# Moving the kernel-tap products of a chunk behind the next chunk's Z groups, in pieces

## The chip, the cores and the metric

The kernel runs on one core of a Trainium2 chip. The time is device time of one execution in microseconds, as a median over runs; the profile is one execution, and its times are counted from the start of its span. Engines are named as in the profile: PE is TensorE (with PEld, its weight loads), DVE VectorE, ACT ScalarE, POOL GpSimd, SP the sync engine, which only issues DMAs.

## The reference

The forward and all gradients of a gated mix of two layers are computed for a sequence of L = 2048 positions, D = 448 channels, with x taken as a constant in the second layer:

```python
g = sigmoid((x * gate_w).sum(-1, keepdims=True))
# a: state space layer, N = 256 states per channel
P = exp(logdA[:, :, None] * l[None, None, :])        # D x N x L
K = einsum("dn,dnl,dn->dl", Cc, P, dB).real          # the taps of a long convolution
y = irfft(rfft(pad(u)) * rfft(pad(K)))[:L] + u * Dskip
# b: squared-ReLU MLP, F = 1792
h = relu(x @ w1 + b1); b = (h * h) @ w2 + b2
out = g * a + (1 - g) * b
```

The outputs are out and the gradients by u, the A, B, C, log_dt and Dskip parameters, w1, b1, w2, b2 and gate_w. What matters here is K: per channel a sum over 256 states of complex powers of one number per state, at 2048 positions; and the way back from dK, the gradient by the taps, to the states.

## The kernel before

**Stages.** Up to about 199 us the kernel loads, does the backward transforms of the convolution and computes dK. From 199 to 628 us a loop goes over the channels in chunks of 32 (`NCH` = 14, with one round more to finish); the MLP's matmuls run beside it. From 628 us the taps K, which the loop has stored to DRAM, are loaded again (L1172), the forward convolution follows (`fwd1`, matmuls at L231), then what is left of the MLP's backward and the weight gradients.

**One chunk.** The position index is split in a product of two tables of powers, X and Y. `x_pair` with `build_x` (VectorE, L762 to L767) makes the X tables of two chunks at once, in rounds with even c. `build_y(c, half)` (VectorE, L774, L775 and L777) makes the Y table in `Ys[c % 2]` by doubling; its operands are broadcast by ScalarE in `expand_y` (L809, L811), those of X in `expand_x` (L804, L805). The K products, `kgen` at L841, are 128 small matmuls per chunk: weights from Y, 128x64, moving data from X, 16 columns, four summed into each place of one PSUM tile `X` (psX). `k_out` (L849, ScalarE) copies the tile into the SBUF buffer KS; at chunks 9 and 13 GpSimd or ScalarE stores KS to DRAM (L855).

For the way back the tables are transposed: X by PE through psX with a ScalarE copy (`tables_t`, L867 and L868), Y by a transposing DMA on SP for three of four groups (`load_yt`, L887), by PE and ScalarE for the fourth (`turn_yt`, L879 and L880) and for the last chunk. `back_z` multiplies the dK block of a chunk (`dk_chunk`, L892) with a transposed Y group: 32 matmuls per group g at L910 into psF, a single buffer, and ScalarE converts the group to bf16 (L914). There are four groups, called Z0 to Z3 here. `back_p` multiplies Z by the transposed X on VectorE, two products of 128x2048 per half (L930), and PE sums them over channels into psS and psN3 (L939). A round c of the loop does Z and P of chunk c−1 and the tables and K of chunk c: K of chunk c is issued in the second half, behind `build_y(c, 1)` and ahead of the transposes of Y and of the second P.

**Beside it.** The MLP's forward hidden layer (`hidden`, L608 and L611, with ScalarE at L613 to L618), its projection (`project`, L1078 and L1080, ScalarE L1081, store L1082), transposes of the weights (L1104, L1115) and the backward through the MLP (`row_block`: L1143 and L1146 on PE, L1148 on ScalarE, product L1155 on VectorE, store L1156 by GpSimd) are issued after the loop in the program, and three of the four row blocks are there to fill the loop's holes.

**What sets the order.** The program is written in the order in which the tensors are produced; a scheduler orders each engine's instructions when the kernel is built, by dependences, priorities and a model of durations, and this order is then fixed. At run time each engine works through its own queue in that order, and waits at an instruction whose input or buffer is not ready. `tc.issue_after(ins)` adds an edge: what is issued in its scope comes behind `ins`. A PSUM tile of one tag (`X`, `S`, `N0` to `N3`, `F`) has one buffer, so that a tile's next use waits for the last reader of the one before. Also Y's two buffers and X's pair of tables may be written again only when K and the transposes of the chunk that they held have been read.

Of the kernel before, what the change touches and what calls it, by code (L numbers as in the profile page):

```python
# [19 lines left out]
P = 128  # L20
# [6 lines left out]
CW = 8  # L27
NG = 4
CC = NG * CW
NCH = D // CC  # L30
# [4 lines left out]
NA = 16  # L35
# [303 lines left out]
def kernel(ctx, tc, A_u, A_A_re, A_A_im, A_B_re, A_B_im, A_C_re, A_C_im, A_log_dt, A_Dskip,  # L339
# [4 lines left out]
    V, S, G_, T_ = nc.vector, nc.scalar, nc.gpsimd, nc.tensor  # L344
# [26 lines left out]
    K = Ker(tc, pool, psum)  # L371
# [140 lines left out]
    ps = K.ps("X", [P, FT + 4], bf16)  # L512
# [43 lines left out]
    th, s, q_ = Lr_, dsa[:, 0:2 * D], dsa[:, 2 * D:4 * D]  # L556
# [26 lines left out]
    ps = K.ps("S", [P, 512])  # L583
# [147 lines left out]
    Ys = [YA[:], KB[:, 6144:14336].rearrange("p (w t b) -> p w t b", t=2, b=64)]  # L731
    XB = K.t("X16", [P, 8192])
    XT5 = XB.rearrange("p (t k w a r) -> p t k w a r", t=2, k=2, w=W2, a=NA)
    XWs = [XT5[:, :, k] for k in range(2)]
# [92 lines left out]
                              PIY[:, k, ws].rearrange("p w t d -> p (w t) d"), rows=rows)  # L827
        return last

    def kgen(c):  # L830
        ps = K.ps("X", [P, 16 * NA])
        for i in range(CW):
            for gg in range(2):
                for jt in range(2):
                    g = 2 * jt + gg
                    ch = 8 * gg + i
                    k = 0
                    for h in range(2):
                        w = g * 16 + h * 8 + i
                        for t in range(2):  # L840
                            T_.matmul(ps[64 * jt:64 * jt + 64, ch * NA:ch * NA + NA], lhsT=Ys[c % 2][:, w, t, :], rhs=XWs[c % 2][:, 1 - t, w, :, 1],  # L841
                                      start=(k == 0), stop=(k == 3), tile_position=(0, 64 * jt))
                            k += 1
        return ps

    def k_out(c, ps):
        cp, cc = c // GC, c % GC
        kv = KS[:, :, cp].rearrange("p a (g q i) -> p q a g i", g=2, q=GC)[:, cc]
        S.copy(kv, ps[:].rearrange("p (g i a) -> p a g i", g=2, a=NA)[:, 0:VA])  # L849
        if c in (9, NCH - 1):  # L850
            c0, c1 = (0, 5) if c == 9 else (5, 7)
            for jt in range(2):
                for (a0, na, st_) in ((0, 2, 1), (2, 2, 2), (4, 2, 1), (6, 6, 256), (12, 1, 1)):
                    nb_ = 1 if a0 == 12 else 64
                    (nc.scalar if jt and c > 9 else G_).dma_start(bass.AP(tensor=k_d, offset=AOFF[a0] * D + 224 * jt + 32 * c0, ap=[[4 * D, nb_], [st_ * D, na], [1, 32 * (c1 - c0)]]),  # L855
                                 KS[64 * jt:64 * jt + nb_, a0:a0 + na, c0:c1].rearrange("p a c e -> p a (c e)"))

    def tables_t(c, gp):
        nonlocal xi
        XT = XTr[xi % 4].rearrange("p (t g n) -> p t g n", g=2, t=2)  # L860
        xi += 1
        pt = K.ps("X", [P, 4, 256], bf16)
        for t in range(2):
            for gg in range(2):
                for h in range(2):
                    w = (2 * gp + gg) * 16 + h * 8
                    T_.transpose(pt[:, 2 * t + gg, h * P:(h + 1) * P], XWs[c % 2][:, t, w:w + 8, :, 0].rearrange("p w a -> p (w a)"), ident[:])  # L867
        S.copy(XT.rearrange("p t g n -> p (t g n)"), pt[:].rearrange("p a n -> p (a n)"))  # L868
        return XT
# [22 lines left out]
        S.copy(DKs[:, c % 2, 0, :, :, 0:VA], src)  # L892
        S.activation(DKs[:, c % 2, 1, :, :, 0:VA], src, ACT.Copy, scale=brow[:, 0:1])

    def back_z(c, YTs, gs):

        nonlocal zi
        cc = c % GC
        DKc = DKs[:, c % 2]
        zb = Zr[zi % 2].rearrange("p (s t g n) -> p s t g n", t=2, s=2, g=2)  # L900
        zi += 1
        for gg, g in enumerate(gs):
            psz = K.psF()
            for s in range(2):
                for par in (1, 0):
                    for ii in range(4):
                        i = 2 * ii + par
                        m = (1 + par) * NA
                        for t in range(2):
                            T_.matmul(psz[32 * ii:32 * ii + m, t, 256 * s:256 * s + 256],  # L910
                                      lhsT=DKc[64 * t:64 * t + 64, s, g, 2 * ii:2 * ii + 1 + par].rearrange("p i a -> p (i a)"),
                                      rhs=YTs[g][64 * t:64 * t + 64, :, i, :], start=True, stop=True, tile_position=(64 * t, 32 * ii),
                                      skip_group_check=True)
            S.copy(zb[:, :, :, gg].rearrange("p s t n -> p t s n"), psz[:].rearrange("p t (s n) -> p t s n", s=2))  # L914
        return zb

    def back_p(c, XT, zb, gs, after):
# [38 lines left out]
    XTs, YTs = {}, {}  # L956
# [63 lines left out]
    for c in range(NCH + 1):  # L1020
        z01 = z23 = None
        if c == 0:
            x_next(0)
        elif c % 2 == 1 and c < NCH:
            XTs[c] = [tables_t(c, 0)]
        if 0 < c < NCH:
            YTs[c] = []
        if c > 0:
            z01 = back_z(c - 1, YTs[c - 1], (0, 1))
        if c % 2 == 1 and c < NCH:  # L1030
            XTs[c].append(tables_t(c, 1))
        if c > 0:
            z23 = back_z(c - 1, YTs[c - 1], (2, 3))
        ap = None
        for half in range(2):
            if c < NCH:
                if c > 0:
                    ay = build_y(c, half, ap or ay)
                if half == 1:
                    k_out(c, kgen(c))  # L1040
                for g in (2 * half, 2 * half + 1) if c > 0 else ():
                    YTs[c].append(turn_yt(c, g) if g == 3 or c == NCH - 1 else load_yt(c, g))
                if c + 1 < NCH:
                    if half == 0:
                        lry = load_ry(c + 1)
                        lry1 = lry if c == 0 else lry1
                        if c % 2 == 1:
                            expand_x(c + 1)
                            expand_x(c + 2)
                        if c == 0:  # L1050
                            expand_y(1, 0, 4)
                    elif c == 0:
                        expand_y(1, 4, 5)
                    else:
                        expand_y(c + 1)
# [42 lines left out]
    for jp in range(FT // 2):  # L1098
        ps = K.ps(NT[ni % 3], [P, 2, D], bf16)
# [8 lines left out]
    for jp in range(FT // 2):  # L1108
        ps = K.ps(NT[ni % 3], [P, DT, 2, P], bf16)
# [292 lines left out]
    gp = const.tile([P, LT], bf16, name="gp")  # L1402
# [121 lines left out]
```

## Time and profile before

| | |
|---|---|
| median of 5 runs | 926.98 us |
| runs | 929.69, 921.80, 932.99, 926.98, 924.27 us |
| the profiled execution | 929.69 us, of which its span is 927.2 us |
| 0 to 199 us (before the loop): PE, DVE, ACT busy | 115.22, 131.99, 131.70 us |
| 199 to 628 us (the loop): PE, DVE, ACT busy | 357.55, 355.59, 316.04 us |
| 628 to 927 us (behind it): PE, DVE, ACT busy | 246.42, 151.68, 144.73 us |
| K products, L841: one; a chunk's 128 | 0.176 us (they overlap); 2.2 to 3.6 us |
| copy of K, L849 | 0.332 us, 14 of them |
| conversion of a Z group, L914 | 1.025 us, 56 of them |
| product for P, L930 | 1.218 us |

How it is read: the page gives busy time over the whole span, and per slice; views of the trace give it for any stretch. A row of the timeline has the start, the duration, engine, line, operation, the tiles written and read, how many instructions were merged, and in brackets how long the engine had been idle before and what ended that. "L930 <- ACT R L914" in the waits reads: VectorE stood at L930 until ScalarE's L914 had written R. Granted clock (PEclk) is the share of TensorE's full clock. Only waits of the engine that is late in a stage cost time.

### The profile page before, as it was taken

Reading aid. Unit: us, or ns where it says so; the run is one execution under the profiler, and the core shown is the slowest. Engines: PE = TensorE matmul, PEld = TensorE weight load, DVE = VectorE, ACT = ScalarE, POOL = GpSimd, SP = SyncE. Lnnn points to the kernel's source line nnn. Section 1 sums busy time; section 2 is a strip of 40 time slices with the busy share of each in tenths; the row PEclk is TensorE's granted clock in tenths of the full one; section 3 lists DMA queues with packets and bytes.
Section 4 is the critical chain, followed back from the end, with each engine's and each line's share of the span. In section 5 each row is a group of like instructions: output and inputs, shape, how many; then the busy total and the mean of one; then the engine's idle time right before and its main releaser. Section 6 shows DMA issues by size and latency. Waiting matters only on the chain.

```text
span 927.2 us, 18872 instructions
## 1 busy us (share of the span) xinstructions
PE 719.2 (78%) x7600; PEld 345.5 (37%) x7633; DVE 639.3 (69%) x1034; ACT 592.5 (64%) x939; POOL 203.4 (22%) x352
## 2 busy tenths in 40 slices
PE   1876744657877877887989779789859869988795
PEld 0332222234334343343553443444323225443353
DVE  4675857696399999989795997933418949759200
ACT  2887768637968968798777836564516645554443
POOL 2341010103112112121221302224213013354120
PEclk8777566577888998897956779999979779989998
DMA  9797675896542656448455576549999988789772
GB/s 238 190 326 266 245 276 220 309 313 168 153 113 72 143 138 156 103 116 148 144 118 111 133 165 157 138 111 301 308 421 275 285 245 254 215 235 273 178 159 62
DMA packets 168238, 184.96 MB, mean 199 GB/s; under 512 B 95347, under 2 KB 145944, under 8 KB 167352
## 3 DMA queue, kind: packets, MB, share of 16 engines
q1 hardware_dynamic: 119062, 83.32, 36.4%
q0 software_dynamic: 21568, 67.46, 22.3%
q10 hardware_dynamic: 27522, 33.00, 11.0%
q8 instruction: 59, 0.97, 0.4%
q14 instruction: 27, 0.22, 0.1%
HBM read 89.60 MB, written 73.13 MB: 175 GB/s over the span
## 4 chain that ended last, share of the span: by engine, by line
PE 34%; ACT 20%; DMA 17%; issue 15%; DVE 9%; POOL 3%; ACTq 1%; POOLq 0%; DVEq 0%; SPq 0%
PE psN L1080 4%; PE psF L1229 3%; DMA R<-Y 3%; DMA S<-rT_d 2%; PE psX L841 2%; PE psF L910 2%; DMA P<-hd 2%; PE psX L879 2%; PE psN L608 2%; PE psN L1229 2%; ACT R L868 2%; DMA rec_d<-F 1%; PE psN L296 1%; ACT R L914 1%; PE psS L939 1%
## 5 line engine op out<-in xcount | busy, mean ns | idle before, releaser
L914 ACT CAST R<-psF 128x1024 bf16<-128x1024 f32 x56 | 57.4, 1025 | 29.3 <-PE psF L910 23.3
L930 DVE TENSOR_TENSOR P<-R 128x2048 bf16<-128x2048 bf16 x42 | 49.5, 1218 | 29.6 <-ACT R L914 29.3
L1229 PEld LDWEIGHTS <-S 128*128 128x128 bf16 x448 | 42.2, 101 | 54.6 <-issue 14.5
L1229 PE MATMUL psF<-U,S 128*128 128x448 bf16 x224 | 52.8, 383 | 2.9 <-ACT S L1224 2.9
L910 PE MATMUL psF<-R,S 64*32 64x256 bf16 (+1 forms) x1344 | 37.2, 311 | 18.5 <-DMA R<-Y 11.7
L1080 PE MATMUL psN<-D,S 128*128 128x448 bf16 x208 | 49.3, 372 | 0.5 <-ACT S L618 0.5
L608 PE MATMUL psN<-S,U 128*128 128x512 bf16 x115 | 39.0, 425 | 11.5 <-ACT M L613 6.1
L774 DVE TENSOR_TENSOR K<-K,F 128x2048 bf16<-128x2048 bf16 (+3 forms) x42 | 36.3, 865 | 10.4 <-ACT F L809 9.1
L775 DVE TENSOR_TENSOR F<-K,F 128x2048 bf16<-128x2048 bf16 (+3 forms) x42 | 35.9, 855 | 7.6 <-ACT F L811 7.6
L209 DVE CAST K<-psN 128x448 bf16<-128x448 f32 x36 | 21.6, 619 | 27.0 <-PE psN L259 25.0
L774 DVE TENSOR_TENSOR Y<-Y,F 128x2048 bf16<-128x2048 bf16 (+3 forms) x42 | 36.4, 866 | 5.2 <-ACT F L809 3.7
L1156 POOL DMA_DIRECT2D dhT_d<-D x28 | 20.4, 729 | 87.5 <-DVE D L1155 79.2
L314 PE MATMUL psN<-P,cb_MI 64*128 64x448 bf16 x128 | 30.0, 408 | 12.0 <-ACT st L208 7.8
L880 ACT COPY M<-psX 128x1024 bf16<-128x1024 bf16 x27 | 27.5, 1017 | 17.2 <-PE psX L879 15.1
L1080 PE MATMUL psN<-S,D 128*128 128x448 bf16 x168 | 37.6, 367 | 0.9 <-DVE D L1155 0.7
L910 PEld LDWEIGHTS <-S 64*32 64x32 bf16 (+1 forms) x1792 | 22.2, 93 | 41.7 <-issue 21.6
L777 DVE TENSOR_TENSOR Y<-Y,F 128x2048 bf16<-128x2048 bf16 (+3 forms) x42 | 36.4, 866 | 1.4
L777 DVE TENSOR_TENSOR K<-K,F 128x2048 bf16<-128x2048 bf16 (+3 forms) x42 | 36.3, 865 | 1.4
L775 DVE TENSOR_TENSOR F<-Y,F 128x2048 bf16<-128x2048 bf16 (+3 forms) x42 | 35.9, 856 | 1.9 <-ACT F L811 1.9
L1143 PE MATMUL psN<-S,U 128*128 128x512 bf16 x114 | 33.0, 391 | 4.1 <-ACT D L1148 2.3
L939 PE MATMUL psS<-P,cb_sel 128*32 128x256 bf16 x224 | 30.3, 340 | 4.0 <-DVE P L930 2.1
L259 PEld LDWEIGHTS <-M 128*64 128x64 bf16 x192 | 13.3, 124 | 50.0 <-issue 45.9
(409 smaller groups left out, 1967.8 us busy)
## 6 DMA issues: line engine op xcount, KB each, us to landing
sp<-K ACTq DMA_DIRECT2D x8, 896.0 KB, 3.6
hd<-st ACTq DMA_DIRECT2D x16, 448.0 KB, 5.0
dhT_d<-D POOLq DMA_DIRECT2D x28, 256.0 KB, 4.7
R<-sp SPq DMA_DIRECT2D x8, 896.0 KB, 22.8
S<-rT_d POOLq DMA_DIRECT2D x14, 512.0 KB, 6.6
R<-hd SPq DMA_DIRECT2D x16, 448.0 KB, 7.9
rT_d<-M POOLq DMA_DIRECT2D x18, 256.0 KB, 3.7
rec_d<-F POOLq DMA_DIRECT2D x2, 1920.0 KB, 10.2
```

What stands on the lines that cost most here:

```text
L314: nc.tensor.matmul(ps[kk2][:, 0:D], lhsT=MI[r0:r0 + 64, ri, :], rhs=sp[r0:r0 + 64, 2 * q2 + ii, ri, :], start=(ri == 0), stop=(ri == 1), t ...
L608: T_.matmul(ps[:], lhsT=w1w[:, dt, j * P:j * P + P], rhs=ub[:, dt], start=(dt == 0), stop=False, skip_group_check=True)
L774: V.tensor_tensor(out=hi, in0=lo, in1=bcast_dims(pr, [0, (None, n // 2), 1]), op=ALU.mult)
L775: V.tensor_tensor(out=Vv.rearrange("p (x a q) -> p x a q", x=rows, q=2), in0=lo, in1=bcast_dims(pi, [0, (None, n // 2), 1]), op=ALU.mult)
L777: return V.tensor_tensor(out=T4[:, :, :, n:2 * n], in0=T4[:, :, :, n:2 * n], in1=V4, op=ALU.add)
L910: T_.matmul(psz[32 * ii:32 * ii + m, t, 256 * s:256 * s + 256], lhsT=DKc[64 * t:64 * t + 64, s, g, 2 * ii:2 * ii + 1 + par].rearrange("p i ...
L914: S.copy(zb[:, :, :, gg].rearrange("p s t n -> p t s n"), psz[:].rearrange("p t (s n) -> p t s n", s=2))
L930: lastp = V.tensor_tensor(out=pr.rearrange("p s t g n -> p s t (g n)"), in0=zv, in1=(xb if r == 0 else rev_dim(xb, 2)), op=ALU.mult)
L939: T_.matmul(sps[s][32 * gr:32 * gr + 32, r, :], lhsT=sel[:, k, off:off + 32], rhs=Q[r][:, s, t, gg, :], start=(g < 2 and cc == 0 and t == ...
L1080: lastm = T_.matmul(ps[:, 0:D], lhsT=hblk[j][:, P * tt:P * tt + P], rhs=ws[:, j, :], start=(w == 1 and j == 0), stop=(j == FT - 1))
L1143: T_.matmul(ps[:], lhsT=w2Tw[:, jp, dt, j % 2], rhs=dblk[:, dt], start=(dt == 0), stop=False, skip_group_check=True)
L1229: lastm = T_.matmul(ps[:, 0:width], lhsT=hh[:, t, :], rhs=(DB2[:, t, :] if w == 0 else U[:, t, 0:D + 1]), start=(t == 0), stop=(t == LT - 1))
```

## The change

`kgen` takes the PSUM tile and a range of the index i, so that it can be issued in pieces. The K products of chunks 1 to 12 go from the second half of their own round into the next round, inside `back_z`: behind the last Z matmul of each group, by an edge. A chunk with even index goes in four pieces of 32 matmuls behind Z0 to Z3, and `k_out` follows after the second pair of groups; a chunk with odd index goes in two pieces of 64 behind Z0 and Z1, and `k_out` follows after the first pair, because the round's `x_pair` rewrites the X tables. The tile psX is taken at the start of the round's Z and is held until `k_out`. Chunks 0 and 13 stay where they were. The second pair of X transposes in odd rounds moves ahead of all Z groups.

```diff
-    def kgen(c):
-        ps = K.ps("X", [P, 16 * NA])
-        for i in range(CW):
+    def kgen(c, ps, i0=0, i1=CW):
+        for i in range(i0, i1):
             for gg in range(2):
                 for jt in range(2):
...
                         for t in range(2):
-                            T_.matmul(ps[64 * jt:64 * jt + 64, ch * NA:ch * NA + NA], lhsT=Ys[c % 2][:, w, t, :], rhs=XWs[c % 2][:, 1 - t, w, :, 1],
+                            lastk = T_.matmul(ps[64 * jt:64 * jt + 64, ch * NA:ch * NA + NA], lhsT=Ys[c % 2][:, w, t, :], rhs=XWs[c % 2][:, 1 - t, w, :, 1],
...
-    def back_z(c, YTs, gs):
+    def back_z(c, YTs, gs, kps=None):
...
-                            T_.matmul(psz[32 * ii:32 * ii + m, t, 256 * s:256 * s + 256],
+                            lastz = T_.matmul(psz[32 * ii:32 * ii + m, t, 256 * s:256 * s + 256],
...
             S.copy(zb[:, :, :, gg].rearrange("p s t n -> p t s n"), psz[:].rearrange("p t (s n) -> p t s n", s=2))
+            if kps is not None:
+                with tc.issue_after(lastz.ins):
+                    if c % 2 == 0:
+                        kgen(c, kps, 2 * g, 2 * g + 2)
+                    elif g < 2:
+                        kgen(c, kps, 4 * g, 4 * g + 4)
         return zb
...
         elif c % 2 == 1 and c < NCH:
-            XTs[c] = [tables_t(c, 0)]
+            XTs[c] = [tables_t(c, gp) for gp in range(2)]
         if 0 < c < NCH:
             YTs[c] = []
         if c > 0:
-            z01 = back_z(c - 1, YTs[c - 1], (0, 1))
-        if c % 2 == 1 and c < NCH:
-            XTs[c].append(tables_t(c, 1))
-        if c > 0:
-            z23 = back_z(c - 1, YTs[c - 1], (2, 3))
+            kps = K.ps("X", [P, 16 * NA]) if 1 < c < NCH else None
+            z01 = back_z(c - 1, YTs[c - 1], (0, 1), kps)
+            if kps is not None and c % 2 == 0:
+                k_out(c - 1, kps)
+            z23 = back_z(c - 1, YTs[c - 1], (2, 3), kps)
+            if kps is not None and c % 2 == 1:
+                k_out(c - 1, kps)
...
-                if half == 1:
-                    k_out(c, kgen(c))
+                if half == 1 and c in (0, NCH - 1):
+                    kps = K.ps("X", [P, 16 * NA])
+                    kgen(c, kps)
+                    k_out(c, kps)
```

More of the change, by code (lines that the diff above doesn't have):

```diff
@@ L840, in kgen @@
                         for t in range(2):
-                            T_.matmul(ps[64 * jt:64 * jt + 64, ch * NA:ch * NA + NA], lhsT=Ys[c % 2][:, w, t, :], rhs=XWs[c % 2][:, 1 - t, w, :, 1],
-                                      start=(k == 0), stop=(k == 3), tile_position=(0, 64 * jt))
+                            lastk = T_.matmul(ps[64 * jt:64 * jt + 64, ch * NA:ch * NA + NA], lhsT=Ys[c % 2][:, w, t, :], rhs=XWs[c % 2][:, 1 - t, w, :, 1],
+                                              start=(k == 0), stop=(k == 3), tile_position=(0, 64 * jt))
                             k += 1
-        return ps
+        return lastk
     def k_out(c, ps):
```

## The prediction

> **What bounds the kernel now.** I read the page's first two parts, then busy time by stretch, then who waits for whom, then the rows round the K products. The page first (busy time, then tenths of 40 slices of 23 us):
>
> ```profile
> PE 719.2 (78%) x7600; PEld 345.5 (37%) x7633; DVE 639.3 (69%) x1034; ACT 592.5 (64%) x939; POOL 203.4 (22%) x352
> PE   1876744657877877887989779789859869988795
> DVE  4675857696399999989795997933418949759200
> PEclk8777566577888998897956779999979779989998
> ```
>
> By the sums TensorE leads; the slices tell another story. The chunk loop fills about 199 to 628 us (slices 8 to 26), and there VectorE carries the nines. Busy time by stretch (columns in the first line):
>
> ```profile
> core 0: us, PE busy (x) PEld busy (x) DVE busy (x) ACT busy (x) POOL busy (x), PEclk, DMA share, GB/s
> 250.00:310.00 60.00, 47.03 (x820) 25.19 (x809) 56.87 (x69) 48.98 (x69) 8.75 (x15) 0.83 0.47 109
> 370.00:430.00 60.00, 52.08 (x806) 26.14 (x808) 55.67 (x66) 49.16 (x68) 10.91 (x18) 0.87 0.53 116
> 430.00:490.00 60.00, 53.49 (x813) 29.79 (x813) 53.63 (x65) 45.77 (x62) 14.43 (x25) 0.76 0.58 132
> 550.00:600.00 50.00, 43.12 (x603) 21.35 (x604) 44.27 (x54) 30.00 (x42) 11.46 (x19) 0.90 0.51 132
> 625.00:927.00 302.00, 248.91 (x1519) 111.62 (x1520) 154.60 (x304) 145.87 (x281) 81.33 (x146) 0.90 0.83 247
> 398.00:402.00 4.00, 3.47 (x154) 3.05 (x152) 2.27 (x6) 3.77 (x8) 0.00 (x0) 1.00 0.21 59
> 470.00:480.00 10.00, 10.00 (x125) 5.60 (x126) 9.72 (x15) 8.40 (x11) 0.00 (x0) 0.50 0.88 173
> ```
>
> VectorE is 93 to 95% busy to 430. From 430 to 490 TensorE is level with it (53.5 against 53.6 of 60). Two chunks take about 58 us, so TensorE has 8 to 14 us of slack per two chunks before 430 and 6.5 after. So in the loop K's place matters only through what VectorE waits for. Its waits from 199 to 625:
>
> ```profile
> DVE P L930 <- ACT R L914: 29.5, 5, 17.0
> DVE D L1155 <- ACT D L1148: 18.9, 7, 8.3
> DVE K L774 <- ACT F L809: 9.1, 3, 5.1
> DVE F L775 <- ACT F L811: 8.6, 7, 1.8
> ```
>
> The first row is the one that K ahead of Z would lengthen. The timeline of VectorE splits it: 17.03 us at 246.7, before any K that moves; 10.56 at 616, in the last chunk, whose K stays; 0.21 at the end. Two waits are left:
>
> ```profile
> 489.26 2.36 DVE L930 TENSOR_TENSOR P<-R 128x2048 bf16<-128x2048 bf16 x2 [0.85 <-ACT R L914]
> 501.62 0.69 DVE L1155 TENSOR_TENSOR D<-D,M 128x1024 bf16<-128x1024 bf16 x1 [8.26 <-ACT D L1148]
> 534.02 0.69 DVE L1155 TENSOR_TENSOR D<-D,M 128x1024 bf16<-128x1024 bf16 x1 [1.59 <-ACT D L1148]
> 556.81 2.36 DVE L930 TENSOR_TENSOR P<-R 128x2048 bf16<-128x2048 bf16 x2 [0.86 <-ACT R L914]
> 563.89 0.69 DVE L1155 TENSOR_TENSOR D<-D,S 128x1024 bf16<-128x1024 bf16 x1 [4.32 <-ACT D L1148]
> ```
>
> And K's own rows, with the waits before them and of those behind them:
>
> ```profile
> 252.64 3.57 PE L841 MATMUL psX<-X,K 128*64 128x16 bf16 x124 [1.91 <-DVE K L777]
> 479.20 3.58 PE L841 MATMUL psX<-X,K 128*64 128x16 bf16 x124
>   ACT R L849: 12.5, 6
> ```
>
> A chunk's 128 products take 2.2 us at clock 1.00 (398.35) and 3.6 at 0.50. ScalarE stands 12.5 us in all for its copy of K (11.5 of it in five waits where K moves), with everything behind it in its queue.
>
> **The change, part by part.** Twelve of 14 K move; work is neither added nor removed (the built order of both kernels has as many TensorE rows, and the same order on SP). The pieces don't come out evenly: in even chunks 96 and 32 products round the last Z group, in odd ones 64 and 64 round the second.
>
> *K leaves the way from the tables to Z.* VectorE's two waits above are all that this can give: 0.85 + 0.86. The first is followed by the 8.26 us wait at 501.62, whose cause is elsewhere, and is lost in it. I take −0.9 (ends −1.7 and 0).
>
> *K now stands ahead of the last Z matmuls.* A Z group's conversion (L914, 1.02 us) then comes up to 96 products later: 1.7 us at full clock, 2.7 at half. Outside the waits above, conversions end 3 to 10 us before VectorE asks (my reading of the timeline), so 0; with that cover gone 6 × 2.7 = 16. VectorE may also not overwrite a Y table before its K is read: the last 32 products (0.6 to 0.9 us) follow Z3, and until the overwrite stand L914 and two L930, 1.0 + 2.4 us. For the X tables 64 products (1.1 to 1.8 us) have the same cover. 0.
>
> *TensorE's hole.* K filled the 2.36 us in which the P sums wait for L930. Now transposes stand there, or nothing. In the even chunks K also covered the landing of the transposing DMA of Y (4.4 to 8.1 us), on which Z waits already (11.7 us in five waits); at chunk 10 Z would come some 1.8 us too early. Between 0 (slack of 6.5 to 14 us) and 6 × 2.36 = 14: nearest is the slack row, I take +0.5.
>
> *ScalarE's order.* L849 goes behind a later L914, two L880 (1.02 us each) now stand round the power expansions L809/L811 for the third table, one L615 (1.0) and one L805 (0.6) more ahead of two later ones: 2.0 + 1.0 + 0.6 = +3.6 for VectorE's L774/L775. Against it, with L849's wait gone, some of their waits at 397 to 456 (1.28 + 1.76 + 2.66 + 1.76 = 7.5) shrink: a third, −2.5. Sum +1 (ends −7 and +4).
>
> *VectorE's order* changes in one thing: the products L1155 of the MLP's backward come later. Those waiting 4.32 and 1.59 us come 6 to 8 us later, while their inputs slip by about 4 us (below); −3.5 (ends −6 and 0). The 8.26 stays.
>
> *Fillers.* MLP matmuls fill TensorE's holes in the built order; up to chunk 9's P sums as many precede as before, behind that fewer, and 19 slip behind the loop (13 of L1143, 6 of L1146). Eight such took 1.73 us at 630.58, 0.216 each: 19 × 0.216 = +4.1. There is no VectorE cover there; the forward convolution waits behind them. The tail is DMA-heavy (share 0.83), which may take some back: ends 0 and 4.1; I take all.
>
> *A wait at the loop's end.* One L231 product, on the K loaded back from memory, now stands in TensorE's queue ahead of some 25 fillers and the 56 L1080; before, it ran behind all of these, at 642.9. Loads land 3.4 to 5.3 us after issue; 0 to 3, I take +1. Queued behind it are those fillers, then L1080.
>
> *Last chunk:* its K stays, but five fillers now precede a transpose ahead of it: +0.4. *Other queues:* GpSimd's stores of K (chunk 9, ten DMAs) come part of an iteration later, their readers are some 50 us off; its other stores shift among themselves. It is 22% busy: 0. SP: 0.
>
> Sum: −0.9 + 0.5 + 1 − 3.5 + 4.1 + 1 + 0.4 = **+2.6**, on the profiled execution's 929.69 us (span 927.2 and 2.5 outside it): 932.3. The median of the runs is 2.7 lower, so 929.6; I say 930.
>
> **The clock.** Four of the moved K (252.64, 479.20, 518.03, 547.19) run at 0.50. [...]
>
> **Rivals.** *A, faster:* ScalarE's freed 11.5 us reach VectorE. Then the waits for expansions in the moved iterations (11.1), the two L1155 (5.9) and the L930 (1.7) go, 18.7, less 4 of fillers and 2 of order: about −12, 915. For it: ScalarE is 82% busy to 430, its queue in order. Against: most of VectorE's lost time isn't behind L849, and L880 and L615 move ahead of expansions.
>
> *B, slower:* the hole. Six even chunks lose 2.36 us each on TensorE, 14 us, that no filler takes: 941. It decides where TensorE's slack for two chunks is below 2.4 us. The profile gives 6.5 or more for the loop, so against; but from 470 to 500 TensorE is busy 29.4 of 30, and fillers slip out behind.
>
> *C, little:* the pieces end up as bursts of 64 to 128 and VectorE's order hardly changes, so nothing but the fillers shows: +4, 931. It lies within my forecast.
>
> **How the numbers follow.** Forecast with C 0.53, A 0.15, B 0.32. Runs of before spread over 921.8 to 933.0, so about 1% (9.3 us) is what can be told from no change. Forecast's own range: cost ends −8 to +8, 919 to 935. The range takes A down to 917 and B up to 944, leaving out under 2 in 10. Faster by over 1% (under 917.7) 0.14, within 0.55, slower (over 936.3) 0.31.
>
> **What would show it.** K in bursts behind Z; L849's waits under 5 us; VectorE's L930 waits from 250 to 600 still under 3; the L1155 waits at 534 and 564 shorter; the last P sums (627.25 before) at 623 to 629, the 56 L1080 starting 5 us later after them. Wrong if L930 waits for L914 in every even chunk or VectorE's share from 250 to 430 falls under 90% (B), or if the loop ends 10 us sooner (A).

## The result, and the profile after

The changed kernel takes 922.66 us in the median of 43 runs, the kernel before 926.32 in 80; the ratio is 0.9942, with a 95% interval of 0.9921 to 0.9964. Ratios here are of fast runs alone, of one kernel those within 1.5% of its own quickest run, so they don't equal the quotient of the medians. The ratio makes 5.4 us of 927, the medians of all runs 3.7: inside the range that the prediction gave, but on the other side of no change than its forecast.

In the changed kernel's file the lines move: K products L840, copy of K L848, Z products L909, conversion L913, product for P L935, MLP product L1164 with its input L1157, projection L1089 and L1090, transposed copies L867 and L879. The page's first two parts:

```profile
PE 723.4 (79%) x7602; PEld 347.7 (38%) x7633; DVE 639.0 (69%) x1034; ACT 593.7 (65%) x939; POOL 203.3 (22%) x352
PE   1876745747886886897899789989859879989795
DVE  4585856597288999999996998833317969659200
PEclk9877565567878899999957679999877778998999
```

Busy time is the same to within 4.2 us on every engine. VectorE's nines stand closer together. A single profile doesn't say how much of that is the change: runs of one kernel spread by some 1.5% either way. So each of the two kernels was profiled twice, and the loop was cut at the starts of VectorE's Y tables (the copies at L822), each round being named by the table that it builds first. Even rounds contain the building of the X tables, odd rounds do not:

| us | before | before, again | after | after, again | mean change |
|---|---|---|---|---|---|
| up to table 2 | 254.8 | 251.8 | 255.4 | 252.1 | +0.5 |
| even rounds, tables 2, 4, 6, 8 | 130.9 | 130.4 | 132.9 | 133.3 | +2.4 |
| odd rounds, tables 3, 5, 7, 9 | 90.6 | 91.4 | 82.8 | 83.6 | −7.8 |
| of that, waits for expansions L809, L811 | 10.0 | 10.9 | 2.2 | 1.5 | −8.6 |
| table 10 to the end of the last P | 150.7 | 147.7 | 143.5 | 144.6 | −5.2 |
| waits for the MLP product in the loop (L1155; L1164 after) | 18.9 | 16.2 | 11.9 | 14.0 | −4.6 |
| behind the last P | 300.2 | 297.1 | 305.1 | 298.2 | +3.0 |
| span | 927.2 | 918.4 | 919.7 | 911.8 | −7.1 |

Stages differ by up to 4 us between two profiles of one kernel, the stretch behind the last P by 7. The odd rounds and their waits differ by more than that, and in both pairs; the stretch from table 10 differs by 3 to 7 us in both pairs, which is hardly clear of the spread. Nor are two profiles of a kernel many: two of one kernel below have odd rounds of 92.3 and 83.4 us. The loop ended, with the last P, 12.4 us sooner in the first pair and 7.8 in the second. The windows of the rounds for tables 7 and 9 before (columns as in the prediction's table of stretches):

```profile
395.86:419.01 23.15, 20.10 (x339) 10.21 (x341) 19.77 (x24) 21.72 (x31) 6.88 (x12) 0.93 0.56 117
451.76:476.29 24.53, 20.78 (x356) 13.30 (x354) 19.77 (x25) 23.07 (x32) 5.24 (x10) 0.83 0.60 142
```

and after:

```profile
398.29:418.40 20.11, 15.73 (x311) 8.26 (x312) 19.66 (x24) 19.18 (x28) 6.70 (x12) 0.97 0.63 145
450.80:471.11 20.31, 18.23 (x308) 11.53 (x307) 19.77 (x24) 17.54 (x24) 5.27 (x10) 0.69 0.69 174
```

VectorE's work in such a round is 19.7 us in both. Before, these two rounds are 3.4 and 4.8 us longer than that, ScalarE is busy for 94% of them, and TensorE has 3 to 4 us left; after, the rounds are 0.5 us longer than VectorE's work. What VectorE waits for from 250 to 600 us in the changed kernel:

```profile
DVE D L1164 <- ACT D L1157: 11.9, 3, 8.9
DVE F L775 <- ACT F L811: 4.6, 4, 1.8
DVE Y L774 <- ACT F L809: 1.1, 1, 1.1
DVE K L774 <- ACT F L809: 0.5, 1, 0.5
```

No wait for a Z conversion is left in that stretch. K's own copy still waits for TensorE, 8.5 us in four waits over the whole span against 12.5 in six, and most of it is one wait:

```profile
547.92 0.33 ACT L848 CAST R<-psX 128x208 bf16<-128x208 f32 x1 [6.00 <-PE psX L840]
548.76 1.01 ACT L913 CAST R<-psF 128x1024 bf16<-128x1024 f32 x1 [0.50 <-PE psF L909]
```

How a wait at an odd table comes about is seen in the timelines of ScalarE and VectorE at table 7. Before:

```profile
389.79 0.54 ACT L1081 CAST D<-psN 128x448 bf16<-128x448 f32 x1
392.19 0.53 ACT L1081 CAST D<-psN 128x448 bf16<-128x448 f32 x1 [1.86 <-PE psN L1080]
392.62 1.15 ACT L804 ACTIVATE F<-recx 128x512 bf16<-128x512 bf16 x2
393.67 1.14 ACT L805 ACTIVATE F<-recx 128x512 bf16<-128x512 bf16 x2
394.71 0.61 ACT L804 ACTIVATE F<-st 128x512 bf16<-128x512 bf16 x1
395.23 1.00 ACT L868 COPY R<-psX 128x1024 bf16<-128x1024 bf16 x1
396.12 1.27 ACT L809 ACTIVATE F<-recy 128x1280 bf16<-128x1280 bf16 x1
397.43 0.41 DVE L774 TENSOR_TENSOR K<-K,F 128x256 bf16<-128x256 bf16 x1 [1.28 <-ACT F L809]
399.59 0.38 DVE L775 TENSOR_TENSOR F<-K,F 128x256 bf16<-128x256 bf16 x1 [1.76 <-ACT F L811]
```

After:

```profile
389.60 0.53 ACT L1090 CAST D<-psN 128x448 bf16<-128x448 f32 x1
390.50 1.15 ACT L804 ACTIVATE F<-recx 128x512 bf16<-128x512 bf16 x2 [0.37 <-DVE X L762]
394.41 1.01 ACT L867 COPY R<-psX 128x1024 bf16<-128x1024 bf16 x1 [1.20 <-PE psX L866]
395.32 1.28 ACT L809 ACTIVATE F<-recy 128x1280 bf16<-128x1280 bf16 x1
398.68 0.40 DVE L774 TENSOR_TENSOR K<-K,F 128x256 bf16<-128x256 bf16 x1
```

Before, ScalarE stands for a projection that TensorE has not finished, and what is behind it in its queue comes late. After, one projection copy fewer is ahead, ScalarE waits for VectorE instead of TensorE at the first X expansion (for TensorE it waits 1.20 us later on), and the table starts without a wait.

### The profile page after: what moved, and what is told of

Same layout as the page of the kernel before. It is cut to its first block, busy times and chain, and to the rows that moved or that the text cites. A ratio compares the mean times of both kernels' runs of the same rounds, so it can differ in the third digit from the quotient of the medians.

```text
span 919.7 us, 18876 instructions
## 1 busy us (share of the span) xinstructions
PE 723.4 (79%) x7602; PEld 347.7 (38%) x7633; DVE 639.0 (69%) x1034; ACT 593.7 (65%) x939; POOL 203.3 (22%) x352
## 4 chain that ended last, share of the span: by engine, by line
PE 35%; ACT 18%; DMA 17%; issue 13%; DVE 13%; POOL 2%; ACTq 1%; SPq 0%; POOLq 0%; DVEq 0%
PE psF L1238 4%; PE psN L1089 4%; PE psX L840 2%; PE psN L1152 2%; DMA hd<-st 2%; DVE F L775 2%; PE psF L909 2%; ACT R L913 2%; DMA P<-hd 2%; PE psN L296 2%; DVE P L935 2%; PE psN L1238 2%; DMA S<-rT_d 2%; DMA rec_d<-F 1%; DMA R<-Y 1%
## 5 line engine op out<-in xcount | busy, mean ns | idle before, releaser
L913 ACT CAST R<-psF 128x1024 bf16<-128x1024 f32 x56 | 57.2, 1022 | 27.4 <-PE psF L909 21.1
L935 DVE TENSOR_TENSOR P<-R 128x2048 bf16<-128x2048 bf16 x42 | 49.5, 1218 | 24.0 <-ACT R L913 23.9
L909 PE MATMUL psF<-R,S 64*32 64x256 bf16 (+1 forms) x1344 | 35.7, 300 | 22.5 <-DMA R<-K 10.1
L1089 PE MATMUL psN<-D,S 128*128 128x448 bf16 x208 | 48.4, 363 | 0.0
L909 PEld LDWEIGHTS <-S 64*16 64x16 bf16 (+1 forms) x1792 | 21.7, 90 | 44.4 <-issue 18.1
L1089 PE MATMUL psN<-S,D 128*128 128x448 bf16 x168 | 36.7, 362 | 1.2 <-DVE D L1164 1.2
L879 ACT COPY M<-psX 128x1024 bf16<-128x1024 bf16 x27 | 27.4, 1013 | 12.1 <-PE psX L878 11.9
L1157 ACT ACTIVATE D<-psN 128x512 bf16<-128x512 f32 x42 | 23.2, 603 | 14.2 <-PE psN L1155 11.0
```

Of the source, the lines that this page charges most:

```text
L879: S.copy(YT[:, h], pt[:])
L909: lastz = T_.matmul(psz[32 * ii:32 * ii + m, t, 256 * s:256 * s + 256], lhsT=DKc[64 * t:64 * t + 64, s, g, 2 * ii:2 * ii + 1 + par].rearra ...
L935: lastp = V.tensor_tensor(out=pr.rearrange("p s t g n -> p s t (g n)"), in0=zv, in1=(xb if r == 0 else rev_dim(xb, 2)), op=ALU.mult)
L1089: lastm = T_.matmul(ps[:, 0:D], lhsT=hblk[j][:, P * tt:P * tt + P], rhs=ws[:, j, :], start=(w == 1 and j == 0), stop=(j == FT - 1))
```

## The experiments

The first theory was that all this is the order of other instructions: the built order has one L1081 fewer ahead of the expansions for tables 7 and 9, and the place of K itself is worth nothing. Its rival: K lies on the way, chunk by chunk. Ratios below are to the kernel before, with 95% intervals; where the medians of all runs say something else, their difference is given too.

### The parts of the change: odd chunks alone, even chunks alone, no splitting

```diff
# against the changed kernel; odd chunks only (even: the same with the other parity)
-            kps = K.ps("X", [P, 16 * NA]) if 1 < c < NCH else None
+            kps = K.ps("X", [P, 16 * NA]) if 1 < c < NCH and c % 2 == 0 else None
...
-                if half == 1 and c in (0, NCH - 1):
+                if half == 1 and (c % 2 == 0 or c == NCH - 1):
```

```diff
# not split
-                    if c % 2 == 0:
-                        kgen(c, kps, 2 * g, 2 * g + 2)
-                    elif g < 2:
-                        kgen(c, kps, 4 * g, 4 * g + 4)
+                    if g == (3, 1)[c % 2]:
+                        kgen(c, kps)
```

> Only the K products of odd chunks move (two pieces, behind Z0 and Z1 of the next round); those of even chunks and the X transposes stay. In its built order ScalarE has the two L880 round the expansions of the third Y table and the L615 ahead of the fourth's, as the changed kernel has, but keeps both projection copies (L1081) ahead of the expansions for the tables 7 and 9; the products L1155 and the fillers behind the loop stand as in the kernel before. Order theory (the gain comes from where the scheduler puts other instructions, above all L1081 ahead of those two expansions, and L1155): no gain, +2 to +4 us against the kernel before, with VectorE's waits at tables 7 and 9 still some 7 us. K theory (the gain comes from K no longer standing between table and P, chunk by chunk): half the change's gain, -2 to -4 us, in small steps at every odd chunk.

> Only the K products of even chunks move (four pieces), with the earlier X transposes that they need. In its built order one L1081 fewer stands ahead of the expansions for tables 7 and 9, no L880 stands round those of the third table, some L1155 come later, and nine fillers more than before stand behind the loop. Order theory: -3.0 and -4.4 us at tables 7 and 9, about -3 at L1155, up to -4 at the last chunk, +2 behind the loop: -6 to -10 us, more than the whole change. K theory: half the change's gain, -2 to -4 us.

> All twelve K move as in the change, but in one block of 128 behind the last Z group that the change uses (Z3 for even, Z1 for odd chunks), so nothing is split. Its built order has both L1081 ahead of the expansions for table 7 and one ahead of those for table 9, L1155 as in the changed kernel, nine fillers more than before behind the loop. Order theory: +3.6 early, -4.4 at table 9, -5 at L1155, -4 at the last chunk, +2 behind the loop: -4 to -8 us, as good as the split form. Split theory (short pieces keep Z and P on time): 128 products in one block delay a Z conversion by 2.2 to 3.6 us, so slower than the changed kernel by 5 us or more and no faster than before.

The odd-only kernel also leaves the second pair of X transposes where it was before; the even-only one moves it as the change does. (Of the edits, the fences show parts.)

Odd chunks alone: 0.9934 (0.9912 to 0.9957), the whole gain. Even chunks alone: 1.0017 (0.9988 to 1.0045), none. Not split: 0.991 (0.988 to 0.9939; medians −5.8 us, where odd-only has −7.5), at least as good as split. The order theory had the first two the wrong way round and falls as it stood: odd-only keeps both copies ahead of the expansions and yet gains. The split theory falls too: splitting is not what helps. Nor are the earlier X transposes, which even-only has and odd-only has not.

### Odd chunks alone, a second profile

> The kernel with only the K of odd chunks moved, once more, for a profile nearer to its median (its first one took 927.4 us, the median is 919.9). The ScalarE theory says that its odd rounds are not shorter than before (90 us or more), so that its gain lies behind table 10 and in the granted clock; if they are at 84 or less here, the first profile misled.

The first profile of odd-only took 927.4 us, 7.5 above that kernel's median, with odd rounds of 92.3 us and 11.6 us of waits in them. The second took 918.6, with 83.4 and 1.2. ScalarE's queue ahead of table 9, first profile:

```profile
448.34 1.01 ACT L913 CAST R<-psF 128x1024 bf16<-128x1024 f32 x1 [0.56 <-PE psF L909]
450.87 0.53 ACT L1092 CAST D<-psN 128x448 bf16<-128x448 f32 x1 [1.52 <-PE psN L1091]
455.27 1.27 ACT L809 ACTIVATE F<-recy 128x1280 bf16<-128x1280 bf16 x1
456.57 0.40 DVE L774 TENSOR_TENSOR K<-K,F 128x256 bf16<-128x256 bf16 x1 [3.53 <-ACT F L809]
```

and second:

```profile
439.94 1.01 ACT L913 CAST R<-psF 128x1024 bf16<-128x1024 f32 x1 [0.31 <-PE psF L909]
442.48 0.53 ACT L1092 CAST D<-psN 128x448 bf16<-128x448 f32 x1 [1.52 <-PE psN L1091]
446.88 1.27 ACT L809 ACTIVATE F<-recy 128x1280 bf16<-128x1280 bf16 x1
449.72 0.41 DVE L774 TENSOR_TENSOR K<-K,F 128x256 bf16<-128x256 bf16 x1
```

The order and every distance within ScalarE's queue are the same: 6.9 us from the Z conversion to L809 in both. Only the moment at which the Z conversion starts against VectorE's table has moved, by some 5 us, and that start was released by TensorE's Z products. So the waits are not fixed by the order of ScalarE's queue; they appear when TensorE reaches Z too late in the even round. A first profile alone would have led the other way.

What differed shows in the even round ahead of table 9 (columns as in the prediction's table of stretches; the third from the end is the granted clock), first profile:

```profile
420.36:452.76 32.40, 27.75 (x399) 13.43 (x401) 31.68 (x40) 21.99 (x31) 3.99 (x6) 0.79 0.67 147
```

and second:

```profile
416.90:449.32 32.42, 29.51 (x445) 14.42 (x445) 31.70 (x40) 26.76 (x38) 4.54 (x7) 0.95 0.63 150
```

The same program was granted a clock of 0.79 in one and 0.95 in the other. Clock in the even round, and VectorE's wait for the expansions of the odd table behind it, in us:

| | clock ahead of table 7 | wait at table 7 | clock ahead of table 9 | wait at table 9 |
|---|---|---|---|---|
| before | 0.89 | 3.0 | 0.79 | 4.4 |
| before, again | 0.83 | 5.1 | 0.95 | 0.7 |
| odd-only | 0.84 | 2.6 | 0.79 | 5.3 |
| odd-only, again | 1.00 | 0.0 | 0.95 | 0.2 |
| after | 0.95 | 0.0 | 0.96 | 0.0 |
| after, again | 0.95 | 0.0 | 0.96 | 0.0 |

In both programs that were granted different clocks the wait goes with the clock. The changed kernel had 0.95 or 0.96 ahead of both tables each time, so part of what separates it from the kernel before may be the clock of its even rounds and not K's place as such. No run held the clock fixed, and which of the two leads is open. The place of K shows in the count over more profiles: of seven with all products done, odd K moved and no other edit to ScalarE's X expansions, six have 0.4 to 3.7 us of these waits in the four odd rounds and one has 11.6 (the first odd-only); five with odd K in place have 7.8 to 10.9.

### The order alone, K in place

```diff
# in project(), the tenth and fourteenth copy
-            S.copy(br, ps[:, 0:D])
+            hold = {9: 7, 13: 9}.get(4 * lb + tt) if w == 0 else None
+            with tc.issue_after(ey[hold].ins) if hold else nullcontext():
+                S.copy(br, ps[:, 0:D])
```

> The kernel before, all K where it was; two projection copies (the tenth and fourteenth L1081) are issued behind the expansions for tables 7 and 9 instead of ahead of them. Order theory: VectorE's waits there (1.28 + 1.76 and 2.66 + 1.76 us) go, -4 to -7 us in the loop without moving K. K theory: nothing, within 2 us, as the waits would come from TensorE being late with K in its way.

0.9964 (0.9937 to 0.9991), −3.3 us (medians −2.3): between the two. The wait at table 9 is gone, but at tables 5 and 7 VectorE still waits (7.8 us in the odd rounds), now with ScalarE standing for the X transposes ahead of the expansions (3.35 and 1.97 us). So part of the gain can be had by order, less than the copies' own waits promised.

### TensorE's time: a quarter of K

```diff
-                    for h in range(2):
+                    for h in range(1):
...
-                        for t in range(2):
+                        for t in range(1):
...
-                                      start=(k == 0), stop=(k == 3), tile_position=(0, 64 * jt))
+                                      start=True, stop=True, tile_position=(0, 64 * jt))
```

> The kernel before with three of four K products left out in every chunk (only the first of each four that are summed is done, so the taps are incomplete); ScalarE's order round the expansions, the L1155 and the fillers behind the loop stand as before. It takes 96 x 14 products off TensorE, 1.7 to 2.7 us per chunk, some 24 us of all K's 31. Cover theory (K's time is hidden, the change gains only by the order of other things): 0 to -2 us. K theory, by odd chunks as the first runs point to (odd chunks' K lies on the way, even chunks' doesn't): -4 to -6 us. If all of K's time lay on the path: -20 us or more.

0.9891 (0.9848 to 0.9934), −10 us (the medians of all runs are 16 us apart): more than the K theory's 4 to 6 us, less than the 20 of all of K's time on the path. The cover theory, and with it the prediction's, is refuted: TensorE's time in K is not all hidden. The waits for the expansions in the odd rounds fall to 1.6 us, and the stretch from table 10 to the last P from 148 to 151 us to 134. Two projection copies still stand ahead of the expansions for tables 7 and 9; but contrary to the expectation the rest did not stay as it was: ScalarE's rows come in another order in many places, and 15 fillers fewer stand between the last P and the forward transform (2 instead of 17), some 3 us at the prediction's 0.216 each.

### The same by kind of chunk

```diff
-                    for h in range(2):
+                    for h in range(1 if c % 2 == 1 else 2):
```

> The kernel before with three of four K products left out in odd chunks only, some 12 us of TensorE. With a quarter of all K done the time fell by 16 us. If K of odd chunks is what makes ScalarE late in the odd rounds: waits there under 3 us, -8 to -12 us. If the even chunks' is: waits of 7 us or more stay, and only what is saved behind table 10 counts, -4 to -6 us.

> The same for even chunks only, some 12 us of TensorE. If K of odd chunks is what makes ScalarE late: waits of 7 us or more in the odd rounds stay, -4 to -6 us. If that of even chunks, which runs right before the odd rounds' expansions: waits under 3 us, -8 to -12 us. If both take the same share, -6 to -10 us each, the place of K inside a round doesn't matter, only TensorE's load.

Odd chunks, in six runs: 0.983 (0.9788 to 0.9872), −16 us (medians −13) for the three quarters of 19.8 us of bursts that it leaves out. Even chunks: 0.9963 (0.994 to 0.9986), −3.4 us (medians −2.2) for three quarters of 18.6. That agrees with the halves of the change: K of odd chunks is on the way, K of even chunks mostly isn't. Neither expectation on the place held: in both profiles VectorE still waited some 8 us for expansions in the odd rounds, and odd's gain stands partly behind the last P (292.4 us against 297 to 300), where its built order has 16 fillers fewer. These two builds changed the order of other instructions too, so the gain can't be put down to K's time alone, and how K of the odd chunks reaches the waits is not shown by them.

### The wait itself: without the odd tables' expansions

```diff
     def expand_y(c, l0=0, l1=5):
+        if c in (3, 5, 7, 9):
+            return
```

> The kernel before without ScalarE's power expansions (one L809 and two L811) for the tables 3, 5, 7 and 9; those tables are then built from the powers of the chunk before, so their values are not the chunk's. VectorE's waits for these expansions (9 us in each of two profiles of the kernel before) cannot occur, and ScalarE, which is 94 to 97% busy in the odd rounds, is relieved of 2.6 us in each. ScalarE theory (in the odd rounds ScalarE's queue is what is late, and the changed kernel gains because this work is done before the round starts): the rounds from table 3 to 4, 5 to 6, 7 to 8 and 9 to 10, 90.6 us together before and 82.8 in the changed kernel, fall to 80 to 84; -5 to -9 us in all. TensorE theory (TensorE is late, the expansions only show it): the wait moves to the Z conversion or the transposed copies behind; the rounds stay at 88 or more, 0 to -3 us.

0.9888 (0.9858 to 0.9918), −10 us (medians −8.7), a little more than the ScalarE theory's. But the profile doesn't place the gain where that theory has it: the odd rounds took 88.7 us together, against 90.6 and 91.4, and not 80 to 84. Three of them are at 20.1 to 21.7 us; the fourth, with 26.9, has a wait of 6.7 us for TensorE's P sums. In this profile the waits moved more than they went; it is of a run of 924.3 us, 6 above its kernel's median, so where the typical run gains is open. That the waits are ScalarE's fault doesn't follow either, as the second profile of odd-only showed.

### ScalarE's queue ahead of the odd tables

```diff
-                            expand_x(c + 1)
-                            expand_x(c + 2)
+                            with tc.issue_after(ey[c].ins):
+                                expand_x(c + 1)
+                                expand_x(c + 2)
```

> The kernel before, all K in place; ScalarE's expansions for the next pair of X tables (L804, L805, five to six of 0.55 us that stand ahead of the expansions for an odd Y table, and that VectorE needs 25 us later) are issued behind those of the Y table. In the built order they do follow; projection copies and an L618 or L613 come ahead instead, and L1155 and the fillers behind the loop stand as in the changed kernel. ScalarE theory (its queue ahead of the expansions is what is late): VectorE's waits there fall from 10 to under 3 us, the odd rounds from 91 to 83 to 85, -4 to -7 us in all without K moved. TensorE theory (ScalarE is only waiting for TensorE there): waits of 7 us or more stay, within 2 us of the kernel before.

> The same edit on the kernel with all K moved in one block each (0.991 of the kernel before). ScalarE theory: the waits are nearly gone there already (3.7 us), so 0 to -3 us more, a ratio of 0.988 to 0.992; nineteen fillers behind the loop instead of nine may take it back. TensorE theory: as that kernel, 0.990 to 0.992.

> The kernel before with ScalarE's X expansions behind those of the odd Y tables, once more. If its gain is the built order's: a ratio of 0.982 to 0.990 again, from table 10 to the last P 134 to 138 us, VectorE's waits for L1155 in the loop 4 to 6 us instead of 16 to 19. If six runs misled: 0.990 to 0.998.

> The same edit on the kernel with only the K of odd chunks moved (0.993). If both gains have their own place (odd rounds, and the stretch behind table 10), they add: 0.976 to 0.983. If they are the same slack taken twice: 0.983 to 0.990.

With K where it was, this edge gave 0.9852 (0.9813 to 0.9891) and, run again, 0.9899 (0.9853 to 0.9944), in six runs each; the medians are 915.96 and 915.86 us. That is quicker than the kernel before both times, and below the changed kernel's 922.66, with which it was not run side by side. The reason given for it was wrong: the waits at the odd tables stay (8.2 and 5.8 us, odd rounds 88.7 and 86.3), and the gain stands behind table 10: 135.5 and 136.4 us to the last P. There VectorE waits little for the MLP's products; its waits from 246 to 640 us in the second profile, whose file has L1157 for the product and L1150 for its input:

```profile
DVE D L1157 <- ACT D L1150: 7.7, 7, 4.8
DVE F L775 <- ACT F L812: 5.7, 4, 1.8
DVE D L1157 <- DMA D<-rT_d: 2.3, 1, 2.3
```

On the unsplit kernel the edge added nothing (0.9912), on the odd-only kernel it gave 0.9894: the gains don't add. Why the edge shortens the stretch behind table 10 was not tested further. The built order lets three projection copies go ahead of the expansions there, and the rest of the MLP may then be reached earlier. The granted clock is a rival: it was 0.852 and 0.838 in the mean of these runs, where the kernel before had 0.831 and 0.827 beside them. The odd-only runs have the same doubt, with 0.842 beside 0.830.

### The long wait for one MLP product

```diff
-                with tc.issue_after(ev.ins):
+                with tc.issue_after(ev.ins), (tc.issue_after(hx[10].ins) if (lb, p_) == (0, 0) else nullcontext()):
                     V.tensor_tensor(out=hb
```

> The kernel before with one product of the MLP's backward, the first L1155, issued behind the end of the X tables of chunk 10 instead of in their midst, where VectorE stood 8.3 us for it. K stays. With it the later L1155 take the places that they have in the changed kernel, and twelve fillers more stand behind the loop (+2.6 us). If VectorE is what is late there: 8 us less in the loop, -4 to -6 us in all. If TensorE is (98% busy from 470 to 500 us), the wait goes to the next product for P and the time changes by less than 2 us.

> The changed kernel with the same edit: the first L1155, for which VectorE stood 8.9 us, behind the end of the X tables of chunk 10. VectorE late: -5 to -9 us against the changed kernel, a ratio to the kernel before of 0.985 to 0.989. TensorE late: within 2 us of the changed kernel, 0.992 to 0.996.

> The kernel before once more, for a second profile. Waits of VectorE that the built order makes (8.3 us at the first L1155, 4.3 at 564, 7.5 at the expansions for tables 7 and 9) show again within 1 us; what differs by more is the run's, and no reading of a single profile on it stands.

0.9998 (0.9953 to 1.0044) and 0.9976 (0.9919 to 1.0033); but the medians of all runs are 922.38 and 922.28 us against 926.15. On the changed kernel (922.66) the edit gained nothing; on the kernel before the two measures are 4 us apart, and whether it gained there is not settled. The wait did not go; in the first of them it became

```profile
484.34 2.36 DVE L931 TENSOR_TENSOR P<-R 128x2048 bf16<-128x2048 bf16 x2 [0.87 <-ACT R L915]
500.59 0.69 DVE L1157 TENSOR_TENSOR D<-D,M 128x1024 bf16<-128x1024 bf16 x1 [6.09 <-ACT D L1150]
503.05 0.69 DVE L1157 TENSOR_TENSOR D<-D,S 128x1024 bf16<-128x1024 bf16 x1 [0.63 <-ACT D L1150]
```

Even behind the X tables VectorE came too early for this product, so its input is what is late there; the wait did not go to the next product for P (0.87 us), as one expectation had it. The second profile of the kernel before had this wait at 5.9 us instead of 8.3, and the waits at tables 7 and 9 as 3.36 + 1.76 and 0.74 us instead of 1.28 + 1.76 and 2.66 + 1.76: their sum, 7.5 and 5.9 us, changes less than their split.

### Behind the loop

```diff
# against the unsplit kernel, in row_block and behind the forward transform
+        if lb == 2:
+            return None
         return project(lb, 1, [hblk[:, j] for j in range(FT)], w1T, [SB[:, 9344 + 448 * k:9792 + 448 * k] for k in range(3)], banks)
...
+    project(2, 1, [hblk[:, j] for j in range(FT)], w1T, [SB[:, 9344 + 448 * k:9792 + 448 * k] for k in range(3)], ["X", "S", "F"])
     lastw = row_block(3, ["X", "S", "F"])
```

> All K moved in one block each, and the projection of the third row block (56 L1080, 10.8 us of TensorE behind the loop) issued after the forward transform of K instead of ahead of it, so that in the built order both are mixed. Path theory (what stands on TensorE ahead of the transform is on the way to the end): the transform starts 8 to 11 us sooner after the last P, -4 to -8 us against the block form alone, a ratio of 0.983 to 0.988 to the kernel before. If the part behind the loop is bound by its DMAs (share 0.83): the start comes sooner, but the time stays within 2 us of the block form, 0.989 to 0.993.

1.0005 (0.9977 to 1.0032), slower than the unsplit kernel's 0.991. TensorE's timeline, unsplit:

```profile
629.00 8.50 PE L1087 MATMUL psN<-S,D 128*128 128x448 bf16 x44 [1.74 <-DVE D L1162]
637.34 0.73 PE L231 MATMUL psN<-X,cb_F1BD 128*128 128x448 bf16 x3
```

and with the projection behind:

```profile
624.72 0.36 PE L231 MATMUL psN<-X,cb_F1BD 128*128 128x448 bf16 x1
630.57 0.54 PE L231 MATMUL psN<-X,cb_F1BD 128*128 128x448 bf16 x2 [1.80 <-DMA X<-k_d]
```

From the end of the last P to the transform's steady rows (637.34 and 630.57) it took 13.1 us instead of 19.4, and from there to the end 290.4 instead of 280.6. The path theory falls as it was put: how soon the transform starts doesn't by itself set the end. The 56 products were moved and not removed, though, so this run doesn't say what TensorE's work behind the loop costs.

## Why the prediction was wrong

**The step that failed** is the one about what bounds the loop, and with it the size of the term *ScalarE's order*. From TensorE's slack of 8 to 14 us for two chunks the prediction took that K could reach VectorE only through the two waits for Z conversions ("all that this can give: 0.85 + 0.86"). But two chunks are an even and an odd round, and they differ. In an even round VectorE has 12 us more to do, the X tables, and there is room; an odd round of the kernel before lasts 21 to 25 us, TensorE has 3 to 4 us left in it and ScalarE about 1. The sum over both hid this. With three quarters of K left out the time fell by 10 us or more, and it is K of the odd chunks that counts: −0.7% for moving it, nothing for moving that of the even ones.

**ScalarE's order** is the term of the sum where this came out. For tables 2 to 4 it had +3.6; the waits there went from 0.19 + 0.83 + 0.90 to 1.09 + 1.80 + 0.47 + 1.76 + 0.55, +3.75, but in the second pair by +1.3 only, so the close agreement is in part luck. The gain was put at a third of 7.5 us. In the first pair all of it went, and table 5's 1.6 too, −9.1; in the second −7.7 with 1.2 left at table 5. Over all tables from 2 to 10 the waits for the expansions went from 11.1 to 6.1 and from 11.9 to 6.0 us: −5.0 and −5.9 where the sum had +1. That alone is most of the distance between the forecast of +2.6 and the measured −3.7 (medians) to −5.4. Its range, from −7 to +4, did hold it.

Rival A's mechanism, waits for the expansions turning into VectorE's time, is what happened, and the loop ended about 10 us sooner (12.4 and 7.8), the sign that the prediction named for it. The reason was another than A's: the copy of K still waits 8.5 us, and what the waits hang on is when TensorE gets to Z. By which instructions K of an odd chunk delays that, and how much of it is the granted clock of the even round, stays open.

**K off the way to Z**: right in kind; the waits of 0.85 and 0.86 us are gone, in the second pair 0.44 and 1.59. **K ahead of the last Z matmuls** and **TensorE's hole**: right that they cost little; no L935 waits for a Z conversion between 250 and 600 us, and TensorE stands still for 54.8 us from 246 to 600 us instead of 60.6 (second pair 50.2 and 60.5). In the last chunk, where K stays, two waits for Z come to 14.2 and 13.3 us instead of 10.8 and 10.5. **L1155**: the waits of the loop fell by 4.6 us in the mean, but not as forecast. The two that were to shrink by 3.5 went from 5.9 to 3.0 us and from 5.6 to 4.4, and the 8.3 us wait that was to stay was 8.3 and 5.9 before, 8.9 and 9.6 after; most of the 4.6 is 4.1 us in the last chunk, where the waits for Z grew. **The wait of L231**: it ran at 617.47 without waiting, 0 instead of +1.

**Fillers and the end**: the 19 stand behind the loop, and the transform starts 21.7 and 21.4 us after the last P instead of 15.9 in both. The stretch behind the last P is 3.0 us longer in the mean, with 7 us between two profiles of the changed kernel. So the 4.1 us are neither confirmed nor refuted.

**The last chunk**: from table 13 to the last P it took 40.7 and 39.7 us, before 42.5 and 41.8, so −2 instead of +0.4.

**The clock**: the sum has no term for it, and over the whole span the mean granted clock is 0.831 after (44 runs) and 0.830 before. By round it differs: the four even rounds have 0.94 and 0.93 in the two profiles after, 0.89 and 0.88 before. Of the moved K at 0.50, the ones at 479.20 and 547.19 stand in stretches at half clock that began behind holes of TensorE of 3.02 us (before 469.24) and 4.67 us (before 544.60); the hole right before the K at 252.64 was 1.91 us.

Rival B did not occur. What stays open besides: why K of the even chunks may move into an odd round without harm but also without gain, and why the X-expansion edge acts behind table 10.

## What to carry to other kernels

Where rounds of a loop alternate, make the table of busy time by round before calling an engine's work hidden: here moving K of the odd chunks into the long rounds gave 0.9934, and moving K of the even ones into the short rounds 1.0017. If a wait's releaser is an in-order queue, look at what that queue was itself waiting for; here two copies held back in ScalarE's queue gave 0.9964 and left 7.8 us of the waits in the odd rounds. And where runs spread by 1%, take two profiles of each kernel before reading a wait of a few microseconds as the kernel's, and compare the granted clock of the stretch ahead of it: two profiles of the odd-only kernel had waits of 5.3 and 0.2 us at table 9, behind even rounds at 0.79 and 0.95.

## What the runs showed of the hardware

The spread between runs goes with the granted TensorE clock. Over 44 runs of the changed kernel the correlation of time and mean granted clock is −0.78, 4.9 us for each 0.01: 908.2 us at 0.859, 935.4 at 0.813. Over 126 runs of the kernel before it is 3.3 us for each 0.01. On a kernel whose page shows VectorE's nines in the loop, that suggests that TensorE is on the way somewhere in the span; a mean over the span doesn't say where, and a correlation doesn't say which causes which.

TensorE was busy throughout in stretches at half clock: from 470 to 480 us all 10.00 us at 0.50 in both profiles of the kernel before. In the first, transposes of the weights (L1104, L1115) take 7.5 of these 10 us; the slow stretch began behind a hole of 3.02 us (a row of TensorE's timeline, then two stretches with the columns of the prediction's table):

```profile
469.24 0.48 PE L1104 MATMUL psN<-ident,U 128*128 128x128 bf16 x3 [3.02 <-ACT S L1105]
465.00:470.00 5.00, 1.98 (x32) 1.28 (x30) 4.97 (x5) 5.00 (x7) 0.56 (x1) 0.77 0.27 77
546.00:556.30 10.30, 10.30 (x195) 6.54 (x194) 9.71 (x11) 3.53 (x5) 0.00 (x0) 0.50 0.28 63
```

The last row is a second such stretch, mostly products of K, the projection, Z and P, with only 2.1 us of transposes (L879). It began behind a hole of 4.67 us (544.60). In both stretches TensorE's row is full for 10 us at half clock, so here a full busy row doesn't show a full clock, and the measured clock decides. What sets the clock was not tested.
